# Second layer by pairs of feature chunks, and the product with the last weight by Strassen's seven block products

## The chip, the core and the metric

The kernel runs on one core of one Trainium2 chip. The metric is the device time of one execution in microseconds; three runs of the kernel before gave 1046.52 to 1047.0, median 1046.98. The engines are named as the profile names them: PE is TensorE (matmuls; PEld its weight loads), DVE is VectorE, ACT is ScalarE, POOL is GpSimd, SP the queue that issues most DMAs.

## What is computed

A channel attention over 6016 tokens of 256 channels feeds two feed-forward layers:

```
x = v @ softmax(normalised kT q / tau)          # 6016 x 256
h = x @ w_in;  g = h * sigmoid(1.702 h);  x = g @ w_out          # first layer, d_ff 2048
gate = sigmoid(x @ w_gate);  val = x @ w_val                     # second layer, d_ff 1536
out = (gate * val) @ w_out2                                      # 6016 x 256
```

The change is in the last two lines.

## The kernel before

**Tiles.** Tokens lie along the free dimension, in 12 blocks of 512 (block 11 has 384). Every fp32 value that goes into a large product is split into two fp16 halves, high and low, and a product is three matmuls (high by high, high by low, low by high) summed in PSUM. The intermediate `x` of a block is split into `vo`; the weights of the gate and the value are in `s_t`, in 12 chunks of 128 features.

**A unit of the second layer.** `gv_unit(b, j)` works on block b and feature chunk j. Gate and value of the chunk are a 2x2 block product (rows: gate, value; columns: the two token halves of w = 256; contraction: the two halves of the 256 channels), and `seven` makes it with seven block products in Winograd's form, so 21 matmuls of w columns. Between them ACT copies partial sums out of PSUM (L1045: one copy into the other bank, two into SBUF, `u2` and `u4`) and DVE adds two of them to the value's bank (L1050). ACT makes the sigmoid (L1408), DVE multiplies (L1414), and the result is split in two fp16 halves, `gh` (L1421 on ACT or L1423 on DVE) and `gl` (L1426 on DVE). The two gate banks come in turns from four (`rot`), the value's from two (`acc` 2 and 3).

**The last weight.** `o_unit(b, j)` multiplies the chunk by its 128 rows of the last weight: two output halves of 128 channels by three matmuls of 512 columns (L1012 to L1014, the helper `prod3`), summed over the 12 chunks of the block in the banks `acc` 0 and 1. After the last chunk ACT copies both banks out with the scale (L1461) and SP stores them (L1466).

**The order.** Nothing runs in the order in which it is written. Each piece of work is given to `Plan.op` with estimated costs, the keys it reads and writes, and the engines that may run it; `Plan.run` then places everything by estimated time and emits it, so each engine's order is fixed when the program is built. A piece with a higher rank number yields to a lower one when both could start; `plan.delay` adds to that rank, and products with the last weight get `FILL2` = 60. In the plan POOL and DVE never run together, except with DVE work marked `lone` (those with an operand in PSUM). Rings (`gf`, `g`: three slots each) bound how far ahead an engine may run. Per block DVE and ACT also prepare `vo` of the next block (`y_ops`, `right_ops`: L310, L313, L359, L362, L365).

Of the kernel before, what the change touches and what calls it, by code (L numbers as in the profile page):

```python
# [166 lines left out]
def fused_kernel(ctx, tc, q, k, vt, tau, w_in, w_o1, w_g, w_v, w_o2, outt):  # L167
# [28 lines left out]
    HSHIFT = VSHIFT = 2.0**-19  # L196
# [1101 lines left out]
    for (b, f0), (nm, src) in zip(W_AT, (("o2", w_o2), ("g", w_g), ("v", w_v))):  # L1298
# [69 lines left out]
    def scales2(e):  # L1368
# [7 lines left out]
        nc.vector.tensor_scalar(ko, ko, w_p2["o2"], 1.0 / TOP / VSHIFT, op0=ALU.mult, op1=ALU.mult)  # L1376
# [4 lines left out]
    def gv_unit(b, j):  # L1381
# [23 lines left out]
        k_g = ring("g")

        def sig(e):
            nc.scalar.activation(  # L1408
                out=T[kf][:, :n].rearrange("p (x w) -> p x w", x=2), in_=pair_ap(kx, w), func=AF.Sigmoid, scale=T[sk]
            )  # L1410

        def mul(e):
            v = T[kf][:, NB : NB + n]
            nc.vector.scalar_tensor_tensor(  # L1414
                out=v, in0=v, scalar=VSHIFT, in1=T[kf][:, :n], op0=ALU.mult, op1=ALU.mult
            )

        def hi(e):
            T[name] = [g_p.tile([P, 2, NB], F16, tag=x, name=x + name)[:, 0, :] for x in ("gh", "gl")]
            if e == "act":  # L1420
# [113 lines left out]
```

## Time and profile before

| | us |
|---|---|
| median of three runs | 1046.98 |
| span of the profiled execution, first to last instruction | 1044.5 |
| busy in that span: PE / DVE / ACT / POOL | 1035.2 / 788.7 / 698.7 / 30.9 |
| first layer's last block ends, second layer's first begins | about 521 to 531 |
| one full block of the second layer | 43.06 |

The profiled execution's own device time is not listed; its span is 2.5 us below the median of the three runs, and this is taken as what lies around it. PE's busy time counts overlapping records, so it shows where PE is never empty, not its speed; that is read from starts of matmuls.

### The profile page before, as it was taken

To read this page: it belongs to the slowest core of one execution; us is meant where nothing else is said; L and a number is where in the kernel's file an instruction comes from. 1 tells how busy PE (TensorE), PEld (TensorE's weight loads), DVE (VectorE), ACT (ScalarE), POOL (GpSimd) and SP (SyncE) were. 2 spreads that over 40 slices of the span, in tenths; PEclk is the share of its full clock that TensorE was granted. 3 is DMA by queue.
4 is the path that set the end of the run, shared out by engine and by line. 5 is a ranking of instruction groups with operands and counts; after the bars stand their busy time and mean duration, and the time that the engine had idled before them with its cause. 6 is when DMAs were issued, how large, how long until landed. Compare 5 with 4: busy or idle time off the path is not lost.

```text
span 1044.5 us, 18259 instructions
## 1 busy us (share of the span) xinstructions
PE 1035.2 (99%) x7169; PEld 715.4 (68%) x7169; DVE 788.7 (76%) x1454; ACT 698.7 (67%) x1387; POOL 30.9 (3%) x39
## 2 busy tenths in 40 slices
PE   9999999999999999999999999999999999999998
PEld 7744456666666666666777777777777777777776
DVE  6999999999888766766686676766767767676665
ACT  6798368787876656655666666666666666666665
POOL 0120100100000000000000000000000000000000
PEclk9999999999999999999999999999999999999999
DMA  9920223300000000000000000000000000000000
GB/s 351 400 104 21 81 78 110 136 23 21 21 2 21 21 2 16 1 1 1 2 2 1 22 1 21 21 1 21 2 21 21 1 21 1 21 21 1 22 21 16
DMA packets 14517, 43.63 MB, mean 42 GB/s; under 512 B 1504, under 2 KB 2784, under 8 KB 12768
## 3 DMA queue, kind: packets, MB, share of 16 engines
q1 hardware_dynamic: 13856, 41.56, 11.0%
q8 instruction: 56, 0.92, 0.4%
q10 hardware_dynamic: 576, 0.92, 0.3%
q14 instruction: 29, 0.24, 0.1%
HBM read 36.31 MB, written 6.16 MB: 41 GB/s over the span
## 4 chain that ended last, share of the span: by engine, by line
PE 93%; DMA 2%; DVE 2%; issue 2%; ACT 1%; POOL 0%; SPq 0%; ACTq 0%; POOLq 0%
PE ps L1036 47%; PE ps L1014 15%; PE ps L1013 15%; PE ps L1012 15%; PE ps L947 1%; DMA tau<-in_tau 1%; DMA m_t<-in_q 1%; PE ps L749 0%; DMA m_t<-in_k 0%; POOL full_in L523 0%; DVE s_t L313 0%; DVE gl L313 0%; DVE full_in L513 0%; DVE big L628 0%; ACT gh L310 0%
## 5 line engine op out<-in xcount | busy, mean ns | idle before, releaser
L1036 PE MATMUL ps<-vo,s_t 128*128 128x256 f16 (+1 forms) x3024 | 370.9, 270 | 0.6 <-ACT m_t L1045 0.6
L1036 PEld LDWEIGHTS <-s_t 128*128 128x128 f16 x3024 | 292.8, 98 | 91.2 <-issue 1.2
L1050 DVE TENSOR_TENSOR gf<-ps,m_t 128x256 f32<-128x256 f32 (+1 forms) x448 | 185.2, 415 | 140.7 <-PE ps L1036 102.9
L1045 ACT COPY m_t<-ps 128x256 f32<-128x256 f32 (+1 forms) x448 | 162.0, 363 | 98.5 <-PE ps L1036 97.1
L1036 PE MATMUL ps<-vo,m_t 128*128 128x256 f16 (+1 forms) x1680 | 217.8, 270 | 0.0
L1036 PEld LDWEIGHTS <-m_t 128*128 128x128 f16 x1680 | 162.6, 98 | 67.8 <-issue 1.0
L1408 ACT ACTIVATE gf<-ps,sgb 128x512 f32<-128x512 f32 (+1 forms) x144 | 97.6, 678 | 66.4 <-PE ps L1036 66.4
L1426 DVE TENSOR_TENSOR gl<-gf,gh 128x512 f16<-128x512 f32 (+1 forms) x144 | 97.9, 680 | 46.1 <-ACT gh L1421 43.5
L1013 PE MATMUL ps<-gl,wo 128*128 128x512 f16 (+1 forms) x348 | 130.2, 374 | 0.0
L1014 PE MATMUL ps<-gh,wo 128*128 128x512 f16 (+1 forms) x348 | 130.2, 374 | 0.0
L1012 PE MATMUL ps<-gh,wo 128*128 128x512 f16 (+1 forms) x348 | 130.2, 374 | 0.0
L1421 ACT CAST gh<-gf 128x512 f16<-128x512 f32 (+1 forms) x132 | 80.4, 609 | 71.7 <-PE ps L1014 71.5
L313 DVE SCALAR_TENSOR_TENSOR gl<-gf,sgi,gh 128x1024 f16<-128x1024 f32 (+1 forms) x87 | 109.0, 1254 | 4.4 <-ACT gh L310 3.8
L1414 DVE SCALAR_TENSOR_TENSOR gf<-gf 128x512 f32<-128x512 f32 (+1 forms) x144 | 98.0, 680 | 13.9 <-ACT gf L1408 0.6
L1013 PE MATMUL ps<-gl,wo_h 128*128 128x512 f16 (+1 forms) x288 | 107.9, 375 | 0.0
L1014 PE MATMUL ps<-gh,wo_l 128*128 128x512 f16 (+1 forms) x288 | 107.9, 375 | 0.0
L1012 PE MATMUL ps<-gh,wo_h 128*128 128x512 f16 (+1 forms) x288 | 107.9, 375 | 0.0
L1045 ACT COPY ps<-ps 128x256 f32<-128x256 f32 (+1 forms) x224 | 82.0, 367 | 16.5 <-PE ps L1036 15.2
L1014 PEld LDWEIGHTS <-wo 128*128 128x128 f16 x384 | 37.6, 98 | 43.6
L1203 DVE TENSOR_SCALAR gh<-gf,sgi 128x1024 f16<-128x1024 f32 (+1 forms) x62 | 45.7, 737 | 27.2 <-PE ps L1014 25.0
L1180 ACT ACTIVATE gf<-gf,sgs 128x512 f32<-128x512 f32 (+1 forms) x80 | 56.0, 708 | 11.5 <-DVE gf L1050 10.6
L1180 ACT ACTIVATE gf<-ps,sgs 128x512 f32<-128x512 f32 (+1 forms) x80 | 53.7, 672 | 9.3 <-PE ps L1036 8.9
(219 smaller groups left out, 982.9 us busy)
## 6 DMA issues: line engine op xcount, KB each, us to landing
v_raw<-in_vt SPq DMA_DIRECT2D x11, 512.0 KB, 5.2
out_t<-ob SPq DMA_DIRECT2D x22, 256.0 KB, 2.0
m_t<-in_k SPq DMA_DIRECT2D x9, 512.0 KB, 6.6
m_t<-in_q SPq DMA_DIRECT2D x9, 512.0 KB, 7.5
s_t<-in_w_o SPq DMA_DIRECT2D x3, 1024.0 KB, 4.9
s_t<-in_w_g SPq DMA_DIRECT2D x3, 1024.0 KB, 5.0
s_t<-in_w_v SPq DMA_DIRECT2D x3, 1024.0 KB, 4.8
big<-in_w_in SPq DMA_DIRECT2D x2, 1024.0 KB, 9.5
```

Source lines behind the costliest of these rows:

```text
L313: nc.vector.scalar_tensor_tensor(out=lo, in0=x, scalar=s, in1=h, op0=ALU.mult, op1=ALU.subtract)
L1012: nc.tensor.matmul(ps[:, :n], w_h, x_h, start=first, stop=False)
L1013: nc.tensor.matmul(ps[:, :n], w_h, x_l, start=False, stop=False)
L1014: nc.tensor.matmul(ps[:, :n], w_l, x_h, start=False, stop=last)
L1036: nc.tensor.matmul(dst, l, r, start=start and y == 0, stop=y == 2, skip_group_check=True)
L1045: op(lambda e: nc.scalar.copy(out=dst, in_=bank(key)[:, :w]), ("act", 0.1 + w / 1150), r=[key], w=[wk], after=after)
L1050: nc.vector.tensor_add(val(half), bank(kw)[:, :w], other)
L1180: nc.scalar.activation(out=dst, in_=pair_ap(kx, w) if x == 0 else dst, func=AF.Gelu_apprx_sigmoid, scale=T[sk][0])
L1408: nc.scalar.activation(out=T[kf][:, :n].rearrange("p (x w) -> p x w", x=2), in_=pair_ap(kx, w), func=AF.Sigmoid, scale=T[sk])
L1414: nc.vector.scalar_tensor_tensor(out=v, in0=v, scalar=VSHIFT, in1=T[kf][:, :n], op0=ALU.mult, op1=ALU.mult)
L1421: nc.scalar.copy(out=T[name][0][:, :n], in_=T[kf][:, NB : NB + n])
L1426: nc.vector.tensor_sub(T[name][1][:, :n], T[kf][:, NB : NB + n], T[name][0][:, :n])
```

## The change

`gv_pair(b, p)` takes two feature chunks (2p, 2p + 1) at once: each of the seven products is made for both chunks into the two halves of one PSUM bank (6 matmuls of 256 columns in a row), and each copy, add and sigmoid works on 512 columns, the product with the gate on 1024. One bank serves all first partial sums (`A_BANK`), one the values (`V_BANK`), and two take turns (`K_BANK`); `acc` 0 to 3 are all left to the last product.

In blocks 1 to 10, `o_pair(b, p)` treats the pair's product with the last weight as a 2x2 block product as well (rows: the two output halves; columns: the two token halves; contraction: the two chunks) and makes it with seven products of 256 columns, summed over the six pairs of a block in seven half banks. For that the pair's result is needed in seven forms: three quarters as they are (`pl`, split by L1548 on ACT and L1551 on DVE) and four sums (`t13`, `t2`, `t4`, `ts` in the trace; L1563, L1566, L1569), split again (L1586, L1589). The four sums of the weight are made once, during block 0 (`o2_sums`). At the end of a block ACT copies the seven sums out (L1687) and seven adds (`comb`, L1695) make the output. Blocks 0 and 11 (`PLAIN2`) keep the product of before, by pairs. `t2`, `t4` and `comb` may run on POOL.

```
-    def gv_unit(b, j):
+    def gv_pair(b, p):
...
+        t = wturn["n"] = 1 - wturn["n"]
+        ka, kx, kw = A_BANK, K_BANK[t], V_BANK
...
+                for f in range(2):
+                    j = 2 * p + f
+                    dst = bank(key)[:, f * w : (f + 1) * w]
+                    lh, ll = [late_pools()["S"][:, j * P // NB, y, a, j * P % NB : j * P % NB + P] for y in range(2)]
+                    for y, (l, r) in enumerate(((lh, rh), (lh, rl), (ll, rh))):
+                        nc.tensor.matmul(dst, l, r, start=start and f == 0 and y == 0, stop=y == 2, skip_group_check=True)
...
+        product(0, 0, ka, True)
+        copy(bank(kx)[:, : 2 * w], ka, kx)
+        product(1, 2, ka, False)
+        product(3, 5, kx, False)
+        copy(u2, kx, ku2)
+        product(4, 4, kw, True)
+        sig(1, ka)
+        product(6, 3, kx, False)
+        copy(u4, kx, ku4)
+        add(0, u4, ku4)
+        product(5, 1, kx, False)
+        product(2, 6, kw, False)
+        add(1, u2, ku2)
+        sig(0, kx)
...
+        op(hi_p, ("act", 0.12 + 0.69 * f), r=rg, w=[kp], after=late_after)
+        op(t13, either(2), r=rg, w=[kt])
+        op(t2, either(1), r=rg + [kt], w=[("t2", name)])
+        op(t4, either(1), r=rg + [kt, ("t2", name)], w=[("t4", name)])
+        op(lo_p, ("dve", 0.12 + 0.81 * f), r=rg + [kp], w=[("plo", name)])
...
+        op(hi_t, ("act", 0.12 + 0.9 * f), r=rt, w=[kg])
+        op(lo_t, ("dve", 0.12 + 1.08 * f), r=rt + [kg], w=[("glo", name)])
...
-    def o_unit(b, j):
+    def o_pair(b, p):
...
+            for x, (a, r, start) in enumerate(((0, 0, True), (1, 2, False), (3, 5, True), (6, 3, False),
+                                               (4, 4, True), (2, 6, False), (5, 1, True))):
+                product(a, r, x, start)
...
+        for k in (0, 3, 1, 2):
+            evac(k)
+        comb(M2, M1, M2)
+        comb(M6, M1, M6)
+        comb(M5, M6, M5)
+        comb(M6, M6, M7)
+        comb(M7, M5, M7)
+        comb(M4, M4, M6)
+        comb(M3, M3, M5)
...
-        for j in range(NF2):
-            gv_unit(b, j)
-            queue2.append((b, j))
+        for p in range(NP2):
+            gv_pair(b, p)
+            queue2.append((b, p))
...
-            elif len(queue2) > 1:
-                o_unit(*queue2.pop(0))
+            elif len(queue2) > LAG2:
+                o_pair(*queue2.pop(0))
...
+            if b == 0 and p >= NP2 - 3:
+                o2_sums(p - NP2 + 3, y_last)
```

Up to the first product of the second layer the order of every engine is the same as before.

DVE, kernel before, around the start of block 4 of the second layer (names carry block, chunk and a buffer number; `tt` and `vo` are `y_ops`):

```order
1008 L1414 SCALAR_TENSOR_TENSOR gf_4_0_7252<-gf_4_0_7252 128x512 [waits DVE_49]
1009 L1426 TENSOR_TENSOR gl_3_11_7286<-gf_3_11_7202,gh_3_11_7285 128x512 [waits Activation_49]
1010 L1050 TENSOR_TENSOR gf_4_1_7303<-ps,m_t 128x256 [waits DVE_49]
1011 L362 TENSOR_TENSOR tt<-big,tt 128x256
1012 L365 TENSOR_TENSOR tt<-big,tt 128x256 [waits DVE_49]
1013 L1050 TENSOR_TENSOR gf_4_1_7303<-ps,m_t 128x256 [waits PE_49]
1014 L1414 SCALAR_TENSOR_TENSOR gf_4_1_7303<-gf_4_1_7303 128x512 [waits DVE_49,Activation_49]
```

The same engine with the change, around the start of block 5 (names carry block and pair):

```order
1033 L1524 SCALAR_TENSOR_TENSOR gf_5_0_7774<-gf_5_0_7774,m_t 128x1024 [waits DVE_49]
1034 L314 SCALAR_TENSOR_TENSOR vo<-big,s_y_203,vo 128x768
1035 L1589 TENSOR_TENSOR gl_4_5_7836<-ts_4_5_7796,gh_4_5_7835 128x1024 [waits Activation_49]
1036 L1563 TENSOR_TENSOR ts_5_0_7870<-gf_5_0_7774 128x512 [waits DVE_49]
1037 L1493 TENSOR_TENSOR gf_5_1_7879<-ps,m_t 128x2x256 [waits Activation_49]
1038 L1551 TENSOR_TENSOR m_t<-gf_5_0_7774,m_t 128x768 [waits Activation_49]
1039 L1569 TENSOR_TENSOR ts_5_0_7870<-gf_5_0_7774,ts_5_0_7870 128x256 [waits Pool_49]
1040 L1493 TENSOR_TENSOR gf_5_1_7879<-ps,m_t 128x2x256 [waits PE_49]
1041 L366 TENSOR_TENSOR tt<-big,tt 128x256
1042 L1524 SCALAR_TENSOR_TENSOR gf_5_1_7879<-gf_5_1_7879,m_t 128x1024 [waits DVE_49,Activation_49]
1043 L1589 TENSOR_TENSOR gl_5_0_7906<-ts_5_0_7870,gh_5_0_7905 128x1024 [waits Activation_49]
```

A pair now takes, beside two adds and one multiplication, the sums `ts` and two splits; here `t2` of pair (5,0) went to POOL, and DVE's `t4` (row 1039) waits for it.

PE with the change, where the first products of pair (5,0) with the last weight stand (`s_t` rows are gate and value products, `m_t` and `gh`/`gl` rows products with the last weight):

```order
10217 L1472 MATMUL ps<-vo,s_t 128x256
10220 L1640 LDWEIGHTS wo_h
10221 L1640 MATMUL ps<-m_t,wo_h 128x256
10222 L1640 LDWEIGHTS wo_h
10223 L1640 MATMUL ps<-m_t,wo_h 128x256
10226 L1640 LDWEIGHTS wo_87
10227 L1640 MATMUL ps<-gh_5_0_7905,wo_87 128x256
10229 L1640 MATMUL ps<-gl_5_0_7906,wo_87 128x256
```

Counting L1472 rows, 42 to a pair, 198 of block 5 stand ahead of row 10227: four pairs and five products of the fifth. The first products from `gl` of pair (5,0) so come 3.7 pairs after that pair's own gate and value products.

POOL with the change, between two blocks (before, POOL had only one cross-partition maximum, L277, left to do in block 0):

```order
63 L1695 TENSOR_TENSOR m_t<-m_t 128x256 [waits DMAHW2_49]
64 L1695 TENSOR_TENSOR m_t<-m_t 128x256 [waits Activation_49]
65 L1569 TENSOR_TENSOR ts_3_3_7100<-gf_3_3_7015,ts_3_3_7100 128x256 [waits DVE_49]
66 L1569 TENSOR_TENSOR ts_3_5_7305<-gf_3_5_7202,ts_3_5_7305 128x256 [waits DVE_49,Activation_49]
67 L1569 TENSOR_TENSOR ts_4_0_7375<-gf_4_0_7299,ts_4_0_7375 128x256 [waits DVE_49,Activation_49]
68 L1566 TENSOR_TENSOR ts_4_1_7440<-gf_4_1_7351,ts_4_1_7440 128x256 [waits DVE_49,Activation_49]
```

All 70 `comb` adds and 37 of the 120 `t2` and `t4` are on POOL.

## Rows read from the trace of the kernel before

**Rows 1.** The page's chain of work that ended last, by engine.

```profile
PE 93%; DMA 2%; DVE 2%; issue 2%; ACT 1%; POOL 0%; SPq 0%; ACTq 0%; POOLq 0%
```

**Rows 2.** What PE waited for, 530 to 1030 us: in total, times, longest.

```profile
PE ps L1036 <- ACT m_t L1045: 0.6, 1, 0.6
```

**Rows 3.** The chain that ended last: start, length, once per block of the second layer.

```profile
595.81 3.61 PE ps L1036 x33
638.87 3.61 PE ps L1036 x33
```

**Rows 4.** Timeline of PE: start, us, what; two stretches without waits.

```profile
552.60 3.77 PE L1036 MATMUL ps<-vo,s_t 128*128 128x256 f16 x33
556.20 0.38 PE L1012 MATMUL ps<-gh,wo_h 128*128 128x512 f16 x1
...
703.52 0.38 PE L1012 MATMUL ps<-gh,wo_h 128*128 128x512 f16 x1
...
704.60 0.38 PE L1014 MATMUL ps<-gh,wo_l 128*128 128x512 f16 x1
```

**Rows 5.** Busy us by stretch: PE, PEld, DVE, ACT, POOL (instructions), clock, DMA.

```profile
160.00:280.00 120.00, 120.00 (x812) 79.14 (x810) 112.32 (x205) 96.38 (x178) 5.17 (x8) 1.00 0.17 56
360.00:480.00 120.00, 120.00 (x813) 79.25 (x811) 83.11 (x155) 72.69 (x142) 4.49 (x7) 1.00 0.02 4
595.80:638.90 43.10, 43.10 (x327) 31.73 (x325) 30.10 (x57) 28.23 (x63) 0.00 (x0) 1.00 0.04 13
```

**Rows 6.** Groups by shape: busy us, mean ns, then idle before.

```profile
L1050 DVE TENSOR_TENSOR gf<-ps,m_t 128x256 f32<-128x256 f32 x408 | 171.0, 421 | 129.1 <-PE ps L1036 97.0 <-ACT m_t L1045 24.6
L1008 DVE TENSOR_TENSOR m_t<-ms,m_t 128x1024 f16<-128x1024 f32 x4 | 4.9, 1216 | 0.0
L359 DVE TENSOR_TENSOR tt<-big 128x512 f32<-128x512 f32 x7 | 4.8, 682 | 0.0
L362 DVE TENSOR_TENSOR tt<-big,tt 128x256 f32<-128x256 f32 x7 | 2.9, 415 | 0.0
L313 DVE SCALAR_TENSOR_TENSOR vo<-big,s_y,vo 128x768 f16<-128x768 f32 x7 | 7.1, 1016 | 0.1
L1408 ACT ACTIVATE gf<-ps,sgb 128x512 f32<-128x512 f32 x132 | 90.6, 686 | 62.2 <-PE ps L1036 62.1
L1007 ACT CAST m_t<-ms 128x1024 f16<-128x1024 f32 x4 | 4.1, 1037 | 9.4 <-DVE ms L988 9.3
```

**Rows 7.** Timeline: two DVE instructions in a row, then a hand-over from PE to ACT to PE.

```profile
704.81 0.49 PE L1036 MATMUL ps<-vo,s_t 128*128 128x256 f16 x3
...
705.22 0.68 DVE L1426 TENSOR_TENSOR gl<-gf,gh 128x512 f16<-128x512 f32 x1
...
705.34 0.37 ACT L1045 COPY m_t<-ps 128x256 f32<-128x256 f32 x1 [0.36 <-PE ps L1036]
...
705.79 1.15 PE L1036 MATMUL ps<-vo,s_t 128*128 128x256 f16 x9
705.83 0.68 DVE L1414 SCALAR_TENSOR_TENSOR gf<-gf 128x512 f32<-128x512 f32 x1
```

**Rows 8.** Timeline near the start: two POOL multiplications, each with DVE's work beside it.

```profile
29.72 2.78 POOL L523 TENSOR_TENSOR full_in<-full_in,big 128x1024 f32<-128x1024 f32 x1 [17.12 <-DVE full_in L513]
...
29.55 3.50 DVE L729 TENSOR_TENSOR kacc<-kacc,sq 128x512 f32<-128x512 f32 x2
...
61.98 2.40 POOL L523 TENSOR_TENSOR full_in<-full_in,raw_in 128x1024 f32<-128x1024 f32 x1 [1.54 <-ACT m_t L310]
...
61.94 4.17 DVE L313 SCALAR_TENSOR_TENSOR m_t<-ps,rss,m_t 128x512 f16<-128x512 f32 x6
```

**Rows 9.** Timeline at the first layer's end, and at the program's end.

```profile
528.28 1.28 ACT L1408 ACT_TABLE_LOAD   x1
...
1038.00 0.33 PE L1012 MATMUL ps<-gh,wo_h 128*128 128x384 f16 x1
...
1040.11 0.33 PE L1013 MATMUL ps<-gl,wo_h 128*128 128x384 f16 x1
```

More of the change, by code (lines that the diff above doesn't have):

```diff
@@ L1357, in fused_kernel @@
             m_sums(SUMS_AT.index(step), [step_op[step]])
+        if b == NBLK - 1:
+            m_users += range(began, len(plan.ops))
         queue.append(step)
@@ L1405, in gv_unit @@
[L1405 to L1409, printed above, removed]
-            )
[L1412 to L1420, printed above, removed]
-                nc.scalar.copy(out=T[name][0][:, :n], in_=T[kf][:, NB : NB + n])
-            else:
-                nc.vector.tensor_copy(T[name][0][:, :n], T[kf][:, NB : NB + n])
@@ new lines, in copy, with quarters, pairs, add @@
+        def copy(dst, key, wk):
+            op(lambda e: nc.scalar.copy(out=dst, in_=bank(key)[:, : 2 * w]), ("act", 0.12 + 2 * w / 1180), r=[key], w=[wk],
+               after=late_after if wk[0] != "rot" else ())
+        def quarters(a, half):
+            return a[:, : 4 * w].rearrange("p (f x w) -> p f x w", f=2, x=2)[:, :, half, :]
+        def pairs(a):
+            return a[:, : 2 * w].rearrange("p (f w) -> p f w", f=2)
+        def add(half, other, ko):
+            def fn(e):
+                if half == 0:
+                    T[kf] = t_p.tile([P, 2 * NB], F32, tag="gf", name="gf" + name)
+                nc.vector.tensor_add(quarters(T[kf], half), pairs(bank(kw)), pairs(other))
+            op(fn, ("dve", 0.12 + 2 * w / 960), r=[kw, ko] + ([] if half == 0 else [kf]),
+               w=[kf] if half == 0 else [("val2", kf)], lone=True)
@@ new lines, in sig, with fn @@
+        def sig(half, key):
+            def fn(e):
+                nc.scalar.activation(out=quarters(sig_t[ks[1] % 2], half), in_=pairs(bank(key)), func=AF.Sigmoid, scale=T[sk])
+            op(fn, ("act", 0.16 + 2 * w / 1180), r=[key, sk] + ([ks] if half == 0 else []), w=[ks] if half == 1 else [("sig2", ks)],
+               after=late_after)
+        u2, u4 = u2_t[:, t, 0, : 2 * w], u2_t[:, t, 1, : 2 * w]
+        product(0, 0, ka, True)
+        copy(bank(kx)[:, : 2 * w], ka, kx)
+        product(1, 2, ka, False)
@@ new lines, in gv_pair, with hi_t @@
+        op(hi_p, ("act", 0.12 + 0.69 * f), r=rg, w=[kp], after=late_after)
[3 more added lines that the diff above has]
+        op(lo_p, ("dve", 0.12 + 0.81 * f), r=rg + [kp], w=[("plo", name)])
+        kg = ring("g")
+        def hi_t(e):
+            T[name] = [g_p.tile([P, 2, NB], F16, tag=x, name=x + name).rearrange("p f n -> p (f n)") for x in ("gh", "gl")]
+            nc.scalar.copy(out=T[name][0][:, : 4 * w], in_=T[kt][:, : 4 * w])
@@ L1480, in fused_kernel @@
             if queue:
-                y_unit(*queue.pop(0))
-                if not queue:
-                    y_max(NBLK - 1)
-                    y_scale(NBLK - 1)
-            elif len(queue2) > 1:
-                o_unit(*queue2.pop(0))
-            if j == 3 and b + 1 < NBLK:
+                began = len(plan.ops)
+                while queue:
+                    y_unit(*queue.pop(0))
+                y_last = list(range(began, len(plan.ops)))
+                y_max(NBLK - 1)
+                y_scale(NBLK - 1)
+            elif len(queue2) > LAG2:
+                o_pair(*queue2.pop(0))
```

225 lines of the change are left out of this document (185 added, 40 removed).

## Prediction

> **What bounds the kernel now.** I read the chain that ended last first: PE holds 93% of it and no other engine has more than 2% [rows 1]; the granted clock is 1.00, the 2.4 GHz level, in every stretch that I read [rows 5]. Next the waits of PE in the second layer: one, of 0.6 us, in 500 us [rows 2]. So PE is full there, and what counts is how fast its matmuls follow each other, not its busy time. The chain passes the same place once per block, 638.87 - 595.81 = 43.06 us apart [rows 3]. Where nothing waits, 33 matmuls of 256 columns start in 556.20 - 552.60 = 3.60 us, 109.1 ns each, and five of 512 columns in 704.60 - 703.52 = 1.08 us, 216 ns each [rows 4]. A block has 12 x 21 = 252 of the first and 12 x 6 = 72 of the second: 27.5 + 15.5 = 43.0 us. The block is its matmuls and nothing else. In the same block DVE is busy 30.10 of 43.10 us and ACT 28.23, POOL not at all [rows 5]: some 30% of room on either, and this is what the change spends.
>
> **PE: what is removed.** Per pair, 42 gate and value matmuls of 256 columns stay as they are, only in runs of six. Twelve matmuls of 512 columns with the last weight (12 x 0.2155 = 2.59 us, by what the period leaves for them) become 21 of 256 columns (21 x 0.1091 = 2.29 us). The new block has 6 x 63 = 378 matmuls of 256 columns, 378 x 0.1091 = 41.24 us, against 43.06: 1.82 us less. Ten blocks (1 to 10) do it: **-18.2 us**. Blocks 0 and 11 keep their matmuls: 0. More than this cannot come out, because the first layer's order is unchanged and PE has no idle time to give back but the 0.6 us of [rows 2].
>
> **ACT: what is added.** Per pair: three PSUM copies and two sigmoids of 512 (0.686 each, the price of the sigmoid), one split of 768 (no row; between the 0.686 of 512 and the 1.037 of 1024, taken as 0.85) and one of 1024 (1.037) [rows 6]: 5.3 us. Six pairs give 31.9; four copies at the block's end (three of 512 and one of 256, by the same prices at most 2.7) and the two splits for the next block (0.85 + 1.04 = 1.9) make 36.5 us, 89% of 41.24. Taken as hidden, since the stretch 160 to 280 us had ACT at 96.38 of 120 and PE lost nothing (below). Cost 0.
>
> **DVE: what is added.** Per pair: two adds of 512 from PSUM (0.42 for 256 in [rows 6]; 512 taken like the SBUF one, 0.68), the multiplication of 1024 (1.216), `t13` of 512 (0.682), `t2` and `t4` of 256 (0.415 each), `lo` of 768 (between 0.682 and 1.216; 0.95) and `lo` of 1024 (1.216): 6.25 us, 37.5 for six pairs. The preparation of the next block adds 0.682 + 2 x 0.415 + 1.016 + 1.216 = 3.7 [rows 6]. The same prices for the block of before (24 x 0.415 + 24 x 0.68 + 3.7) give 30.0, and [rows 5] shows 30.10, so I trust them. From 41.2 I take what the order puts on POOL, 37 x 0.415 / 10 = 1.5: **39.7 us** of records per block. Records overlap by some 0.07 us when the next instruction does not wait (a 0.68 us one is followed after 0.61 [rows 7]); with about 50 instructions a block the true need lies between 36.2 and 39.7 us, 88 to 96% of 41.24.
>
> Can PE stay full beside a DVE that busy? The trace has that case. From 160 to 280 us DVE is busy 112.32 of 120 us (94%) and PE starts 812 matmuls; from 360 to 480 us DVE is at 83.11 (69%) and PE starts 813 [rows 5]. The mix is the first layer's in both. So a static order of this planner held PE full at 94%, and I take DVE's added work as hidden.
>
> **POOL beside DVE.** This the trace of before does not show in the second layer. Each block gets 7 adds and 3.7 `t2` or `t4` of 256 elements. The nearest row is a POOL multiplication of 1024, 2.78 us, and it ran beside two DVE adds whose records took 3.50 us together [rows 8], where two such take 2 x 0.682 = 1.36: DVE stood still for some 2.1 us, nearly POOL's whole work. A second one, 2.40 us, ran beside six DVE splits that read PSUM, and these kept their pace, 4.17 / 6 = 0.70 us each for 512 elements. So DVE work with an operand in PSUM is not held up. A quarter of 2.78 us is 0.70 for 256 elements; with a fixed part it is more, and 0.75 is my estimate, bounded by 0.52 (a quarter of the 2.1) and 2.78 (no gain from fewer elements). 10.7 x 0.75 = 8.0 us of POOL per block. DVE is delayed by nothing, if all of it falls on DVE's PSUM adds (12 x 0.68 = 8.2 us a block) or its idle time, and by 8.0 us if none does. By this, DVE needs 38 + 0 to 8 = 38 to 46 us, with PE at 41.24. The planner kept the two engines apart in its order, so that DVE's instructions stand where it expected POOL to be done; I take a collision cost that reaches PE of 0.25 us per block, **+2.5 us**, and keep 0 and 46 - 41.2 = 4.8 us per block as the ends.
>
> The Trainium skill, "SBUF — State Buffer", section "Who interferes with whom", says that a VectorE instruction with two SBUF inputs contends with a GpSimd instruction that reads SBUF, and that one with at most one SBUF input does not. The 3.50 us agree with the first half and the 4.17 us with the second. By that rule alone every sum, split and multiplication of the new block can be held up and only the adds cannot, so the end with 8.0 us is the one to fear: 1077, worked out with the rivals.
>
> **Banks.** One bank now carries all first partial sums and one all values. The value's circle for a pair is product, add, product, add, 4 x 0.67 = 2.7 us, with four hand-overs. PE's three matmuls from 704.81 end at 705.30, ACT starts its copy at 705.34, ends at 705.71, and PE starts again at 705.79 [rows 7], so a hand-over is below 0.1 us where the receiver is free: 3.1 us of the 6.87 us that a pair takes. The circle decides only when DVE answers on average 0.9 us late. Taken as 0.
>
> **The slack of the last product.** Between a pair's last gate product and its products with the last weight lie add, multiplication, `t13`, `t2`, `t4`, `hi` and `lo`: 0.68 + 1.22 + 0.68 + 0.42 + 0.42 + 1.04 + 1.22 = 5.7 us, 6.4 with seven hand-overs. In the order they stand 3.7 pairs later for pair (5,0), 25 us. So PE has ready work in hand, and a late `lo` does not stop it; a late add does.
>
> **The start.** The last four feature chunks of the first layer now lie between products of the second in longer runs, and the load of the sigmoid's table (1.28 us on ACT [rows 9]) has copies for PE queued behind it; of it 0.6 us reached PE before. I add **+1 us** (0 to 3). The weight's sums in block 0 are 3 x (1.216 + 4 x 0.415 + 1.216) = 12.3 us on DVE, in a block whose own work is 6 x 3.8 + 3.7 = 26.5 of 43: hidden; without that room it would be at most 12.3.
>
> **The end.** Block 11's last product is as before, and 57 of its matmuls (13 of 384 columns in 1040.11 - 1038.00 = 2.11 us [rows 9], 0.162 each, 9.2 us) stand behind the last gate product, which needs add, multiplication and split, about 4 us. Cost 0. Stores go in four pieces of 128x256 per block, on a queue with little to do: 0.
>
> **The sum.** 1044.5 - 18.2 + 2.5 + 1 = 1029.8 us of span; with the 2.5 us by which the median of the runs lies above the span, **1032.3 us**.
>
> **Rivals.** *POOL and DVE collide for about half of POOL's work* (4 us): DVE needs 38 + 4 = 42 us a block, with the odd wait on top 42.3; the ten blocks give 10 x 0.76 = 7.6 back, and with +1 the time is 1040.4. For it: 8 us of POOL in a block with 3 us of spare DVE time. Against: the plan's own separation.
>
> *DVE becomes the bound and the kernel is slower.* Place: every block from 1 to 10, where the adds that free the value's bank queue behind held-up splits. It decides when more than 43.06 - 38 = 5.1 of POOL's 8 us hold DVE up, about two thirds. At three quarters it is 44 us a block, +9.4, and 1057; with all of it 46 us, 1077. For it: in [rows 8] nearly all of POOL's time was lost to DVE. Against: 8.2 us of adds from PSUM in a block that could lie beside POOL.
>
> *Single banks.* The Trainium skill, "Perfetto Trace Analysis", section "Matmuls", asks that independent groups rotate through different PSUM banks. As a mechanism of this kernel: if each of the 66 pairs of blocks 0 to 10 loses 0.3 us until the previous pair's second add has emptied the value's bank, 20 us go, and the time is 1052; at 0.1 us, 1039. Against it stand the 3.7 us of slack in the circle.
>
> **How the numbers follow.** Forecast (PE bound, 1028.8 to 1036): 0.58. Half collided (1036 to 1045): 0.20. DVE bound (1046 to 1077): 0.16. Banks (1036 to 1055): 0.06. The range 1028.5 to 1045 holds the first two and half of the last, 0.81. About 0.2%, 2.1 us, is what a measurement of this kernel can tell from no change. Faster: 0.58 + 0.20 + 0.02 = 0.80. Slower: 0.13 of the third case and 0.02 of the last, 0.15; the same: 0.05.
>
> **What would show it.** In the changed profile: blocks 41.3 to 41.6 us apart in PE's order, 378 matmuls of 256 columns in each; PE's waits below 0.5 us a block; DVE at 88 to 96% of a block, ACT at 84 to 89%, POOL at about 8 us. DVE records of `lo` or `ts` much longer than 1.22 and 0.42 us beside a POOL add would show the collision; waits of PE on DVE's L1493 that add up to over 1.8 us a block would make the prediction wrong. Waits at the first layer's end of more than 3 us would show the start mis-sized.

## The result and the profile after

The changed kernel takes 1027.76 us (median of four runs, 1027.24 to 1029.05); before took 1046.99 beside it. The ratio is 0.9819, with a 95% interval of 0.9807 to 0.9831, a gain of 19.2 us. The profiled execution took 1027.24 us, with a span of 1025.2 us. The forecast was 1032.3; the time lies 0.7 us below the lower end of its range. Most kernels here have single executions with a mean granted clock of 0.998 instead of 1.00 that take some 2 us longer (1029.05 against 1027.24 to 1028.10 here), so up to 2 us of a difference between two medians of four can be that.

The page of the changed kernel: busy time by engine, then the chain that ended last by engine (as [rows 1]), then the groups of the second layer's work. L1472 are the gate's and value's products, L1640 the seven block products of the last weight, L1493 DVE's two adds that read PSUM, L1480 ACT's copies out of PSUM, L1500 its sigmoids, L1695 the combinations.

```profile
PE 1016.8 (99%) x7709; PEld 767.9 (75%) x7709; DVE 875.7 (85%) x1377; ACT 736.6 (72%) x1193; POOL 122.2 (12%) x145
...
PE 91%; DVE 3%; DMA 2%; issue 2%; ACT 1%; POOL 0%; SPq 0%; ACTq 0%; POOLq 0%
...
L1472 PE MATMUL ps<-vo,s_t 128*128 128x256 f16 (+1 forms) x3024 | 362.0, 270 | 0.2 <-ACT m_t L1500 0.2
L1493 DVE TENSOR_TENSOR gf<-ps,m_t 128x512 f32<-128x512 f32 (+1 forms) x144 | 97.3, 676 | 37.2 <-PE ps L1472 31.8
L1480 ACT COPY m_t<-ps 128x512 f32<-128x512 f32 (+1 forms) x144 | 83.0, 576 | 38.7 <-PE ps L1472 34.7
L1695 POOL TENSOR_TENSOR m_t<-m_t 128x256 f32<-128x256 f32 x70 | 65.5, 949 | 67.3 <-ACT m_t L1687 65.1
```

What PE waited for in the second layer (in total, times, longest), as [rows 2], and the busy time of PE, PEld, DVE, ACT and POOL, as [rows 5]: the whole second layer, then two stretches inside it.

```profile
PE ps L1472 <- ACT m_t L1500: 0.2, 1, 0.2
...
521.68:1021.63 499.95, 499.70 (x4505) 436.37 (x4502) 444.34 (x607) 373.99 (x568) 92.03 (x107) 1.00 0.04 13
...
650.00:814.00 164.00, 164.00 (x1505) 147.00 (x1503) 150.19 (x204) 127.00 (x192) 36.39 (x42) 1.00 0.04 14
814.00:980.00 166.00, 165.99 (x1523) 148.66 (x1522) 151.28 (x203) 127.48 (x193) 35.95 (x41) 1.00 0.04 14
```

The second layer of before, from its first gate product to its last product:

```profile
521.53:1040.60 519.07, 518.44 (x3965) 383.55 (x3962) 357.63 (x684) 336.46 (x762) 0.64 (x1) 1.00 0.03 12
```

So the second layer went from 519.07 to 499.95 us, 19.1 less, and what lies around it from 525.4 to 525.2. The view of waits has PE waiting for 0.2 us in it. In the eight blocks of the two stretches DVE is busy 301.47 of 330 us (91%), ACT 254.49 (77%) and POOL 72.34, or 9.0 us in a block of 41.3.

The feared collision is there. The timeline of POOL, then that of DVE, at the end of a block:

```profile
922.71 3.94 POOL L1695 TENSOR_TENSOR m_t<-m_t 128x256 f32<-128x256 f32 x3
...
921.97 1.75 DVE L314 SCALAR_TENSOR_TENSOR vo<-tt,s_y,vo 128x1024 f16<-128x1024 f32 x1
923.64 1.75 DVE L1589 TENSOR_TENSOR gl<-ts,gh 128x1024 f16<-128x1024 f32 x1
925.30 0.68 DVE L1493 TENSOR_TENSOR gf<-ps,m_t 128x512 f32<-128x512 f32 x1
```

And a place without one:

```profile
934.11 0.73 POOL L1566 TENSOR_TENSOR ts<-gf,ts 128x256 f32<-128x256 f32 x1 [6.78 <-ACT m_t L1500]
...
933.88 0.68 DVE L1493 TENSOR_TENSOR gf<-ps,m_t 128x512 f32<-128x512 f32 x1
```

A POOL add of 256 elements takes 0.73 us beside a DVE add that reads PSUM, and neither is stretched. Of the three in the 3.94 us above, the first two lie beside DVE's work in SBUF and take 1.59 us each, the third lies beside L1493 and takes 0.72; `lo` (L1589) takes 1.75 instead of 1.22: 0.53 more. That is about the lower of the two bounds that the prediction set for one such add (0.52, a quarter of the 2.1 of [rows 8]). PE loses next to nothing by it. Why not is what the experiments are about.

### The profile page after: what moved, and what is told of

The parts are those of the page before. It is cut to its first block, busy times and chain, and to the rows that moved or that the text cites. A ratio compares the mean times of both kernels' runs of the same rounds, so it can differ in the third digit from the quotient of the medians.

```text
span 1025.2 us, 18922 instructions
## 1 busy us (share of the span) xinstructions
PE 1016.8 (99%) x7709; PEld 767.9 (75%) x7709; DVE 875.7 (85%) x1377; ACT 736.6 (72%) x1193; POOL 122.2 (12%) x145
## 4 chain that ended last, share of the span: by engine, by line
PE 91%; DVE 3%; DMA 2%; issue 2%; ACT 1%; POOL 0%; SPq 0%; ACTq 0%; POOLq 0%
PE ps L1472 31%; PE ps L1037 17%; PE ps L1640 13%; PE ps L1015 10%; PE ps L1014 10%; PE ps L1013 10%; PE ps L948 1%; DMA tau<-in_tau 1%; DVE gl L314 1%; DMA m_t<-in_q 1%; DMA m_t<-in_k 1%; DVE vo L314 0%; POOL full_in L524 0%; DVE gf L1051 0%; DVE s_t L314 0%
## 5 line engine op out<-in xcount | busy, mean ns | idle before, releaser
L1472 PE MATMUL ps<-vo,s_t 128*128 128x256 f16 (+1 forms) x3024 | 362.0, 270 | 0.2 <-ACT m_t L1500 0.2
L1472 PEld LDWEIGHTS <-s_t 128*128 128x128 f16 x3024 | 292.6, 98 | 38.2 <-issue 0.6
L1493 DVE TENSOR_TENSOR gf<-ps,m_t 128x512 f32<-128x512 f32 (+1 forms) x144 | 97.3, 676 | 37.2 <-PE ps L1472 31.8
L1500 ACT ACTIVATE m_t<-ps,sgb 128x512 f32<-128x512 f32 (+1 forms) x144 | 97.5, 680 | 41.4 <-PE ps L1472 40.5
L314 DVE SCALAR_TENSOR_TENSOR gl<-gf,sgi,gh 128x1024 f16<-128x1024 f32 (+1 forms) x87 | 109.1, 1255 | 4.2 <-ACT gh L311 3.6
L1046 ACT COPY m_t<-ps 128x256 f32<-128x256 f32 (+1 forms) x160 | 57.5, 364 | 74.4 <-PE ps L1037 73.2
L1480 ACT COPY m_t<-ps 128x512 f32<-128x512 f32 (+1 forms) x144 | 83.0, 576 | 38.7 <-PE ps L1472 34.7
L1051 DVE TENSOR_TENSOR gf<-ps,m_t 128x256 f32<-128x256 f32 (+1 forms) x160 | 65.3, 414 | 42.6 <-ACT m_t L1046 25.6
L1524 DVE SCALAR_TENSOR_TENSOR gf<-gf,m_t 128x1024 f32<-128x1024 f32 (+1 forms) x72 | 88.2, 1229 | 1.9
L1589 DVE TENSOR_TENSOR gl<-ts,gh 128x1024 f16<-128x1024 f32 x60 | 74.4, 1241 | 3.4 <-ACT gh L1586 3.3
L1640 PEld LDWEIGHTS <-wo 128*128 128x128 f16 x720 | 70.3, 98 | 8.0
L1640 PE MATMUL ps<-gh,wo 128*128 128x256 f16 x360 | 76.1, 273 | 0.0
L1695 POOL TENSOR_TENSOR m_t<-m_t 128x256 f32<-128x256 f32 x70 | 65.5, 949 | 67.3 <-ACT m_t L1687 65.1
L1015 PEld LDWEIGHTS <-wo 128*128 128x128 f16 x384 | 37.6, 98 | 43.6
L1586 ACT CAST gh<-ts 128x1024 f16<-128x1024 f32 x60 | 62.7, 1046 | 6.1 <-DVE ts L1569 3.6
```

The costliest lines, as they stand in the source:

```text
L314: nc.vector.scalar_tensor_tensor(out=lo, in0=x, scalar=s, in1=h, op0=ALU.mult, op1=ALU.subtract)
L1015: nc.tensor.matmul(ps[:, :n], w_l, x_h, start=False, stop=last)
L1472: nc.tensor.matmul(dst, l, r, start=start and f == 0 and y == 0, stop=y == 2, skip_group_check=True)
L1480: op(lambda e: nc.scalar.copy(out=dst, in_=bank(key)[:, : 2 * w]), ("act", 0.12 + 2 * w / 1180), r=[key], w=[wk], after=late_after if wk[0 ...
L1493: nc.vector.tensor_add(quarters(T[kf], half), pairs(bank(kw)), pairs(other))
L1500: nc.scalar.activation(out=quarters(sig_t[ks[1] % 2], half), in_=pairs(bank(key)), func=AF.Sigmoid, scale=T[sk])
```

## The experiments

Theory A: PE is the bound throughout, and what the change adds to DVE, ACT and POOL is hidden, collisions included. Against it stand a gain that comes from elsewhere (the pairs and their full banks), collisions that do reach PE, and a DVE that is the bound itself.

**pairs_only.** What the pairs do without Strassen's products.

```diff
-T_BY, T_PEN, E_BY, E_PEN, LAG2, PLAIN2 = ("dve", "pool"), 0.0, ("dve", "pool"), -1.0, 2, (0, 11)
+T_BY, T_PEN, E_BY, E_PEN, LAG2, PLAIN2 = ("dve", "pool"), 0.0, ("dve", "pool"), -1.0, 2, tuple(range(12))
```

> The changed kernel with all 12 token blocks on the plain products (PLAIN2 = all blocks): pairs of features on full banks stay, Strassen's products do not run (the weight sums of block 0 are still formed). Theory A (TensorE is the bound throughout; the columns of the products with the last weight are what the change saves, and the pairs take away only the short stalls of the last block, 0.7 us, and 0.4 us at the layer's start): 1045.5 to 1046.3 us, blocks 43.0 to 43.1 us apart. Rival B (the pairs themselves give a share of the gain of 19 us, through fuller banks): below 1042. Rival C (the start costs 1 us, as the prediction's sum had it): 1048.

1045.25 us, ratio 0.9985 (0.9976 to 0.9993) to before: 1.8 us less, 0.25 us more than A's expectation allowed; nearly all of the gain is the products'. The second layer of this kernel:

```profile
522.69:1040.28 517.59, 517.35 (x3965) 383.56 (x3962) 322.21 (x403) 325.47 (x488) 0.35 (x1) 1.00 0.03 12
```

It is 519.07 - 517.59 = 1.5 us shorter than in before, and Strassen's products take away another 517.59 - 499.95 = 17.6 us, 1.76 in each of ten blocks. Where half of the 1.5 us was, the timeline of PE shows in block 11, first before, then the changed kernel: twelve products of 192 columns.

```profile
1026.68 1.24 PE L1036 MATMUL ps<-vo,s_t 128*128 128x192 f16 x12
```

```profile
1010.24 1.15 PE L1472 MATMUL ps<-vo,s_t 128*128 128x192 f16 x12
```

PE lost 0.09 us inside such a run and waited for nothing that the view of waits names: it leaves short waits out. All that PE loses can be read from the starts of its products. A stop is the time by which the step from one product to the next is longer than in an unbroken run (0.109 us for 256 columns, 0.0825 for 192, 0.162 for 384, 0.216 for 512). In the second layer the stops add up to 1.89 us in before, 0.41 in pairs_only and 0.63 in the changed kernel. So they are the whole 1.5 us: the one at the layer's start (the wait of 0.6 us of [rows 2]) went from 0.79 to 0.40, nine in block 11 with 0.77 together are gone, and so are two at 667 and 789 us with 0.28 together.

**no_pool and all_pool.** Everything that may go to either engine on DVE alone, then on POOL alone (the first and the second new line); the planner makes a new order for each.

```diff
-T_BY, T_PEN, E_BY, E_PEN, LAG2, PLAIN2 = ("dve", "pool"), 0.0, ("dve", "pool"), -1.0, 2, (0, 11)
+T_BY, T_PEN, E_BY, E_PEN, LAG2, PLAIN2 = ("dve",), 0.0, ("dve",), -1.0, 2, (0, 11)
+T_BY, T_PEN, E_BY, E_PEN, LAG2, PLAIN2 = ("pool",), 0.0, ("pool",), -1.0, 2, (0, 11)
```

> The changed kernel with every addition of the second layer on VectorE (no GpSimd). VectorE is busy 37.6 us of 41.1 in a block of the changed kernel; some 3.4 two-input additions of 0.42 us and 7 of 0.42 us per block come to it, and about 1 us of lengthened instructions goes, so about 41 us of 41.3. Theory A (collisions with GpSimd are hidden, VectorE's remaining slack is what is spent): 1028 to 1034 us, with TensorE waits for VectorE's parts in some blocks. Rival D (collisions of GpSimd with VectorE do reach TensorE in the changed kernel): faster than the changed kernel by 1 to 2.5 us, 1025 to 1027.

> The changed kernel with all four differences of a pair and all seven combinations on GpSimd (120 + 60 + 70 additions instead of 34 + 70): GpSimd some 24 us of a block instead of 9, VectorE about 30 us of its own work. Theory A (a GpSimd addition beside VectorE's two-input work stretches both, but both lie in slack): 1027 to 1029.5 us. Rival D (collisions reach TensorE as the prediction's sum had it, 2.5 us per 8 us of GpSimd a block): +7 us, about 1035; as its rival had it, 1045 and more. A second way to lose under A: the chain of a pair becomes longer than the slack of the last product, which shows as TensorE waits on line 1640 for VectorE or ScalarE.

no_pool took 1033.78 us, 6.0 more than the changed kernel, inside A's expectation: without POOL there is no collision, and it is slower all the same. PE's waits there are not for DVE's parts, as expected, but for ACT's copies (2.4 of 2.8 us listed from block 1 on). all_pool took 1047.50, 19.7 more, which A did not expect. What PE waited for in all_pool, from block 1 on, and POOL's groups between 650 and 980 us:

```profile
PE ps L1472 <- ACT ps L1480: 7.0, 4, 1.8
PE ps L1472 <- DVE gf L1493: 3.1, 8, 0.7
PE ps L1640 <- DVE gl L1589: 2.1, 4, 0.5
...
L1563 POOL TENSOR_TENSOR ts<-gf 128x512 f32<-128x512 f32 x46 | 78.4, 1705 | 73.8 <-DVE gf L1524 35.6 <-ACT m_t L1480 17.6 <-ACT m_t L1500 11.1
L1566 POOL TENSOR_TENSOR ts<-gf,ts 128x256 f32<-128x256 f32 x45 | 53.7, 1193 | 3.1
```

So POOL's work does reach PE when there is more of it. Load, collisions and order change together here; the next runs take them apart.

**dve_more1, load_only, plan_only.** A quarter of a pair's last split is made twice. dve_more1 has both edits below; load_only has the first alone, so that the planner doesn't know and every engine keeps the changed kernel's order; plan_only has the second alone.

```diff
         def lo_t(e):
             nc.vector.tensor_sub(T[name][1][:, : 4 * w], T[kt][:, : 4 * w], T[name][0][:, : 4 * w])
+            nc.vector.tensor_sub(T[name][1][:, : 1 * w], T[kt][:, : 1 * w], T[name][0][:, : 1 * w])
...
-        op(lo_t, ("dve", 0.12 + 1.08 * f), r=rt + [kg], w=[("glo", name)])
+        op(lo_t, ("dve", 0.12 + 1.08 * f + 0.12 + 1 * 0.27 * f), r=rt + [kg], w=[("glo", name)])
```

> The changed kernel with a quarter of the low part of a pair's differences formed twice on VectorE (one more 128x256 subtraction, 0.42 us, in each of 60 pairs; the result is unchanged): VectorE 37.6 + 2.5 = 40.1 us of a block of 41.3. Theory A (what is not TensorE's work is hidden up to a full engine): no change, 1027.5 to 1028.7 us. Rival E (VectorE's slack is already used up where it matters, in the last steps of a pair): +0.42 us for each pair, about 1053, or a good part of it, above 1033.

> dve_more1's extra subtraction (0.42 us on VectorE in each of 60 pairs), but with the planner told the old duration, so that the order of all instructions on all engines is the changed kernel's. It tells the load of dve_more1 (1051.8 us, +24 on the changed kernel) from the other order that the planner made of it. Theory F (the slack of VectorE is smaller than the 0.42 us per pair, since it stands still for TensorE's banks within the pair: VectorE and TensorE hand work to each other in turn): 1045 to 1053 us, nearly +0.42 us per pair. Theory G (the order of dve_more1 cost the time; VectorE's 3.5 idle us a block take 2.5 more): 1028 to 1032 us.

> The counterpart: the planner is told 0.42 us more for that subtraction, as in dve_more1, but the subtraction is not doubled; the order moves, the work is the changed kernel's. Theory F (load): 1027 to 1031 us. Theory G (order): 1045 us or more.

dve_more1 took 1051.82 us (+24.1), load_only 1040.13 (+12.4), plan_only 1042.46 (+14.7). A failed here, in the form in which DVE's idle time is its room: 0.42 us a pair is 2.5 of the 3.6 us in which DVE stands idle in a block, and in load_only half of it reached PE. Neither F nor G held either: the load alone and the order alone each cost some 13 us. PE's waits from block 1 on, in load_only, then in plan_only:

```profile
PE ps L1472 <- DVE gf L1493: 6.3, 12, 1.4
PE ps L1472 <- ACT m_t L1500: 0.5, 1, 0.5
```

```profile
PE ps L1472 <- ACT m_t L1500: 6.1, 8, 1.0
PE ps L1640 <- DVE m_t L1551: 1.6, 7, 0.2
```

In load_only PE waits for the adds that free the value's bank, the wait that the prediction named as the one to look for. The view lists half of it: by the starts of its products PE stops for 12.8 us in all, 10.2 of them until such an add has ended. In plan_only, with the changed kernel's work (only three `t2` went from POOL to DVE), a sigmoid and the splits come too late. It happens at one place in each of seven blocks and costs some 2 us each time, here at 770 us (DVE, ACT, PE):

```profile
767.04 1.28 DVE L314 SCALAR_TENSOR_TENSOR vo<-tt,s_y,vo 128x1024 f16<-128x1024 f32 x1
...
769.48 0.83 ACT L1548 CAST m_t<-gf 128x768 f16<-128x768 f32 x1 [1.49 <-DVE gf L1524]
770.22 0.68 ACT L1500 ACTIVATE m_t<-ps,sgb 128x512 f32<-128x512 f32 x1
...
770.96 0.82 PE L1472 MATMUL ps<-vo,s_t 128*128 128x256 f16 x6 [0.96 <-ACT m_t L1500]
```

The multiplication L1524 stands behind DVE's L314, which prepares the next block; the split L1548 waits for it, and the sigmoid that PE needs stands behind that split on ACT. The order of the changed kernel is therefore part of its time: another one, made by the same planner from one duration that was 0.39 us longer, loses 14.7 us.

**load_half and load_double.** The dose at the changed kernel's order: 128 elements (the first line) and 512 (the second) in place of load_only's 256.

```diff
+            nc.vector.tensor_sub(T[name][1][:, : w // 2], T[kt][:, : w // 2], T[name][0][:, : w // 2])
...
+            nc.vector.tensor_sub(T[name][1][:, : 2 * w], T[kt][:, : 2 * w], T[name][0][:, : 2 * w])
```

> As load_only (the changed kernel's order on every engine), with an extra VectorE subtraction of 128x128 instead of 128x256 in each of 60 pairs: by the step from 256 to 512 elements (0.42 to 0.68 us) about 0.28 us. Theory H (VectorE has a slack of fixed size in each pair and beyond it every nanosecond counts; load_only's +12.4 us for 60 x 0.42 us makes it 0.21 us a pair): +4 us, about 1032. Rival I (no slack: a share of about half of any load on VectorE reaches TensorE): +8 us, about 1036.

> As load_only, with an extra subtraction of 128x512 (0.68 us) in each of 60 pairs. Theory H (a slack of 0.21 us a pair): 60 x 0.47 = +28 us, about 1056. Rival I (half of the load): +20 us, about 1048.

1032.86 and 1055.14 us, near H's 1032 and 1056. The records of the extra instruction are 0.292, 0.425 and 0.692 us long, and the next DVE instruction starts 0.209, 0.343 and 0.610 us after it (medians). The three kernels are 5.1, 12.4 and 27.4 us over the changed kernel, which is 0.085, 0.206 and 0.456 us for each of 60 pairs. The difference is 0.124, 0.137 and 0.154 us. The second layers alone, which the medians hold beside everything else, in the same order:

```profile
523.77:1027.69 503.92, 501.57 (x4505) 436.28 (x4502) 462.36 (x667) 374.08 (x568) 96.74 (x107) 1.00 0.04 13
...
522.74:1034.84 512.10, 504.53 (x4505) 436.08 (x4502) 472.57 (x667) 374.89 (x568) 97.38 (x107) 1.00 0.04 13
...
523.79:1051.70 527.91, 507.71 (x4505) 435.99 (x4502) 489.50 (x667) 375.20 (x568) 98.92 (x107) 1.00 0.04 12
```

They are 3.97, 12.15 and 27.96 us longer than the changed kernel's 499.95, which is 0.066, 0.203 and 0.466 us a pair, and the difference is 0.143, 0.140 and 0.144: the same for all three doses. So DVE has some **0.14 us of slack a pair** at this place and in this order, 0.8 us in a block, and beyond it every nanosecond counts. Its 3.6 idle us a block are not slack. More than half of them it waits for PE's products, 16.2 of 28.5 us from 650 to 980 us in the changed kernel:

```profile
DVE gf L1493 <- PE ps L1472: 16.2, 22, 1.6
```

**pe_less.** What the next saving on PE would bring; this kernel leaves out the low-weight term of three of the seven block products.

```diff
-                    for y, (l, r) in enumerate(((lh, rh), (lh, rl), (ll, rh))):
+                    terms = ((lh, rh), (lh, rl), (ll, rh))[: 2 if x in (0, 2, 4) else 3]
+                    for y, (l, r) in enumerate(terms):
...
```

> What the next saving of the same size on TensorE would bring: the third of the three 16-bit terms is left out of three of the seven block products (18 of 126 products with the last weight a block, so the output loses accuracy); the order of what is left is the changed kernel's. TensorE: 18 x 0.1093 = 1.97 us a block less, 19.7 us in ten blocks. Theory A alone (TensorE is the only bound): about 1008 us. Theory H (VectorE has 0.21 us of slack a pair, 1.3 us a block, and becomes the bound): about 1015 us. Rival I (VectorE and TensorE in turn, half reaches): about 1018 us.

1014.49 us: 13.3 of 19.7 us came out, near H's 1015. That is 1.3 us a block, where the doses leave 0.8, and what holds PE back then is not DVE alone:

```profile
650.00:814.00 164.00, 163.45 (x1489) 145.32 (x1488) 155.74 (x212) 132.05 (x200) 38.43 (x43) 1.00 0.04 14
```

DVE went from 150.19 to 155.74 of 164 us, 95%, and ACT from 127.00 to 132.05. By the starts of its products PE stops for 5.8 us behind the layer's start: 2.9 of them end with one of DVE's adds L1493, and 2.7 with a copy or a sigmoid of ACT, which mostly stand behind ACT's own splits. H's number came out, its bound only in half.

**pool_twice.** POOL's additions done twice (`t2` and the combinations are shown, `t4` is done likewise; `dump` is a scratch tile) at the unchanged order of the other engines.

```diff
+            if e == "pool":
+                nc.gpsimd.tensor_sub(s(2), q(2), s(0))
             eng(e).tensor_sub(s(2), q(2), s(0))
...
+                if eg == "pool":
+                    nc.gpsimd.tensor_add(dump[:, :w], e(a), e(c))
```

> Each of GpSimd's additions of the second layer done twice (34 of a pair's differences and 70 combinations; the second copy of a combination goes to a scratch tile), with the planner told nothing, so that the order on TensorE, VectorE and ScalarE is the changed kernel's: GpSimd some 18 us of a block instead of 9, twice the collisions with VectorE. Theory A (GpSimd's collisions with VectorE are hidden by slack): no more than +2 us, 1028 to 1030. The prediction's step (0.25 us per block for 8 us of GpSimd): +2.5 us, about 1030. Rival D (they reach TensorE once the slack is used): VectorE loses about as much as it lost already in the changed kernel, 0.8 us a block, against a slack of 1.3: still about 1028 to 1030 by H; with no slack, 1036 and more.

1077.25 us, 49.5 more than the changed kernel: every theory missed by far. The waits of PE, the longest one of ACT from block 1 on, and the timeline of POOL, then of DVE and ACT, at one place (line numbers are up to seven higher; L1473 are the gate's and value's products, L1481 the copies, L1574 is `t4`, L1591 the high part, L1494 the adds):

```profile
PE ps L1473 <- ACT m_t L1481: 18.9, 20, 4.1
PE ps L1473 <- DVE gf L1494: 13.5, 13, 2.4
...
ACT gh L1591 <- POOL ts L1574: 34.1, 20, 4.8
...
907.59 0.72 POOL L1573 TENSOR_TENSOR ts<-gf,ts 128x256 f32<-128x256 f32 x1 [4.29 <-DVE ts L1569]
908.39 1.59 POOL L1574 TENSOR_TENSOR ts<-gf,ts 128x256 f32<-128x256 f32 x1
...
908.15 1.25 DVE L1525 SCALAR_TENSOR_TENSOR gf<-gf,m_t 128x1024 f32<-128x1024 f32 x1
909.32 0.94 DVE L363 TENSOR_TENSOR tt<-big,tt 128x256 f32<-128x256 f32 x1
910.01 1.05 ACT L1591 CAST gh<-ts 128x1024 f16<-128x1024 f32 x1 [2.75 <-POOL ts L1574]
```

The first `t4` falls beside the PSUM add and takes 0.72 us. The second meets the multiplication L1525, takes 1.59, and the DVE instruction behind takes 0.94 in place of 0.42. But that is not what costs most: ACT waits 2.75 us for POOL with the high part, and its copies that free PE's banks stand behind it in its queue. DVE's low part waits for that high part in turn (19.0 us from 650 to 980 us), with adds behind it. (The granted clock was 0.99 and 0.98 in the two stretches of that time, worth at most some 5 of the 49.5 us.) So a late POOL add costs by what queues behind its reader; the changed kernel shows ACT waiting 2.5 us for `t4` in all. This run doesn't tell what a collision costs, and the next two were made for that.

**no_comb and no_comb_load.** The seven combinations of a block are cut to two of 256 columns, in the changed kernel and in load_only (most of the output's combination is left out).

```diff
-                (nc.gpsimd if eg == "pool" else nc.vector).tensor_add(e(out), e(a), e(c))
+                (nc.gpsimd if eg == "pool" else nc.vector).tensor_add(e(out)[:, :2], e(a)[:, :2], e(c)[:, :2])
```

> GpSimd's seven combinations of each of ten blocks are cut to two columns of 256 (most of the output's combinations are left out); the order on TensorE, VectorE and ScalarE is the changed kernel's. It takes away the collisions that stretched VectorE's instructions by some 9.5 us in ten blocks of the changed kernel. Theory H (TensorE is the bound there and the collisions lie in VectorE's slack): no change, 1027.3 to 1028.5 us. Rival D (collisions reach TensorE): 1018 to 1025 us.

> The same cut in load_only (0.42 us more on VectorE in each of 60 pairs, 1040.1 us). There the combinations stretched VectorE's instructions by 15.7 us in ten blocks. Theory H (beyond the slack every microsecond on VectorE counts, a stretched one too): most of load_only's 12.4 us comes back, 1028 to 1032 us. Rival J (the stretched instructions stand where VectorE would have waited for TensorE anyway, so a collision costs nothing even when VectorE is the bound): 1038 to 1040 us.

no_comb took 1027.37 us, its span is 1025.2 us as in the changed kernel. Its DVE:

```profile
650.00:814.00 164.00, 164.00 (x1505) 147.00 (x1503) 146.64 (x205) 126.94 (x192) 18.71 (x42) 1.00 0.04 14
814.00:980.00 166.00, 166.00 (x1525) 148.83 (x1523) 146.70 (x203) 127.50 (x193) 19.40 (x41) 1.00 0.04 14
```

DVE is busy 293.34 us with the same instructions that took 301.47: the combinations stretch them by 8.1 us in eight blocks, 1.0 a block, and PE hardly notices: its only stop that goes with them is one of 0.17 us, behind an L1493 at 963 us. The 36 `t2` and `t4` on POOL are still there; none of them takes longer than 0.735 us in the changed kernel. no_comb_load took 1031.74, 8.4 us less than load_only: where DVE has no slack left, the combinations cost 0.84 us a block, about half of the 15.7 us in ten blocks by which they stretch DVE's instructions there. So they have a price, and the changed kernel pays it out of slack. H holds, D and J don't.

**last_block and lag1.** A version that might have been faster (the first new line), and one with less slack (the second).

```diff
-T_BY, T_PEN, E_BY, E_PEN, LAG2, PLAIN2 = ("dve", "pool"), 0.0, ("dve", "pool"), -1.0, 2, (0, 11)
+T_BY, T_PEN, E_BY, E_PEN, LAG2, PLAIN2 = ("dve", "pool"), 0.0, ("dve", "pool"), -1.0, 2, (0,)
+T_BY, T_PEN, E_BY, E_PEN, LAG2, PLAIN2 = ("dve", "pool"), 0.0, ("dve", "pool"), -1.0, 1, (0, 11)
```

> The changed kernel with Strassen's products in the last block of 384 tokens too (PLAIN2 = block 0 alone). TensorE's columns: 72 products of 384 columns (0.1625 us) become 126 of 192 (0.0825 us), 11.7 - 10.4 = 1.3 us less. The end: the changed kernel has 3.6 us from the last product to the end of the span; with the combinations one ScalarE copy and up to three additions (0.33 us each at 192 columns) stand before the last store instead of the one copy, about +1 us. Theory A: 1026.5 to 1028.3 us, no change to a gain of 1 us. A rival (the combinations stand on the tail with all seven additions and the slow ones on GpSimd): 1029 to 1031 us.

> The changed kernel with the products of the last weight one pair behind the gate's products instead of two (LAG2 = 1). The prediction put the slack of these products at 3.7 pairs. If a slack of that size is there, 1027.5 to 1029 us. If the chain of a pair (sigmoid 0.68, product 1.23, differences 0.68 + 0.42 + 0.42, high part 1.05, low part 1.24, together 5.7 us of a pair's 6.9 without any queueing) uses it, TensorE waits on line 1640 in most pairs, 1 us or more each: above 1060 us.

last_block took 1036.83 us, 9.1 more. Its last block, PE's longest waits at the end of it, then its end in the chain that ended last:

```profile
980.62:1027.20 46.58, 42.42 (x452) 39.15 (x450) 39.48 (x60) 29.68 (x53) 9.95 (x13) 0.98 0.05 15
...
PE ps L1640 <- DVE gl L1589: 1.6, 2, 0.8
PE ps L1640 <- ACT gh L1586: 0.9, 2, 0.5
...
1026.29 0.59 ACT m_t L1687
...
1027.01 0.60 POOL m_t L1695
...
1029.59 1.09 POOL m_t L1695 x2
```

The block takes 46.6 us where the changed kernel takes 40.8 from its first gate product to the last product. Most of that is lost behind the last gate product, which ends at 1019 us: the products of the last pairs wait for their high and low parts, six stops with 4.6 us together, and no gate product is left to lie between. (In the last 3.2 us of the block the granted clock was 0.64, too.) Then five combinations on POOL stand one behind the other at the end: the span ends 6.2 us after the last product, not 3.6. My expectation had left the first out altogether, and the second was its rival. lag1 took 1030.13 us, 2.4 more. PE waits 0.2 us on L1640 in it, so the slack of the last product is there, as the prediction had it. The longer waits are for ACT's copies, 0.9 us, in an order that the planner made anew; how much of the 2.4 us is the order's is not shown.

## Why the prediction was right in direction and too high

| term of the sum | predicted, us | measured, us | from |
|---|---|---|---|
| span before | 1044.5 | 1044.5 | |
| products of ten blocks on PE | -18.2 | -17.6 | pairs_only to the changed kernel, second layer |
| pairs: start, block 11, elsewhere | +1, 0, 0 | -0.4, -0.8, -0.3 | before to pairs_only, stops of PE in the second layer |
| POOL beside DVE | +2.5 | 0 (at most 0.2, within the -17.6) | no_comb: same span |
| before and behind the second layer | 0 | -0.2 | spans less second layers |
| span after | 1029.8 | 1025.2 | |
| outside the span | 2.5 | 2.0 | the profiled execution; the median is 0.5 above it |

**The bound** was read rightly: PE is full in the second layer, before and after, and its matmuls' time is the gain. The products' -18.2 was 0.6 too much: 256-column products start 0.1093 us apart on average in the changed kernel's second layer (3988 pairs of starts), not 0.1091, which is 0.08 us in the 378 of a block; the 43.06 us that they were set against were measured.

**The step that failed in the sum is the term for POOL beside DVE**, +2.5. The collision happens, at 1.0 us of DVE a block and about the price of one add that the bound gave. What reached PE was 0.2 us at most in the whole layer. I compared DVE's need with PE's 41.24 us and then took a value between the ends that no row supported; no_comb and no_comb_load show the price and that slack covers it. The rival with half of POOL's work collided had the stretching four times too large (4 us a block) and falls; so does the slower one. The Trainium skill, "SBUF — State Buffer", section "Who interferes with whom", held in both halves: beside L1493, which reads one operand from PSUM, a POOL add kept its 0.73 us, and beside two-SBUF work both engines were held up.

**The second failed step** is "More than this cannot come out ... PE has no idle time to give back but the 0.6 us". The view of waits leaves short ones out; block 11 had stops of 0.09 us in PE's own row, which the pairs' order doesn't have, and outside the start they were 1.05 us in all. With it the start's +1 had the wrong sign: the stop there shrank from 0.79 to 0.40 us. This step and the collisions are 2.5 us each of the 4.6 by which the span was forecast too long; the products' 0.6 goes the other way.

**Banks**: the rival falls; PE waits 0.2 us in the whole layer. **DVE**: 88 to 96% predicted, 91% measured, and the reading behind it (hidden, because 94% was hidden at 160 to 280 us in [rows 5]) came out right by 0.14 us a pair, which was luck. It was not safe: load_only at 95 to 96% loses 12.4 us and plan_only loses 14.7 with the changed kernel's work. A busy share in another stage said nothing about where DVE's instructions stand in this one. The check of DVE's prices was in part chance as well: 30.0 is a sum of records, 30.10 is busy time, which counts overlaps once, and the records of that block add up to 31.3. **ACT**: 84 to 89% predicted, 77% measured. A PSUM copy of 512 takes 0.585 us and I had priced it like the sigmoid, 0.686, which is 1.9 of the 4.7 us a block; most of the rest is overlap, since the records add up to 34.4 us a block and the busy time is 31.8. **POOL**: 8.0 us a block predicted, 9.0 measured, the difference being its own stretching (36 `t2` and `t4` ran on it by the trace, not 37).

What stays open: why pe_less finds 1.3 us of slack a block where the doses find 0.8, and what lag1's 2.4 us are made of.

## What to carry to other kernels

Beside a full engine, the idle time of another is not its slack. Put a small extra instruction into the inner loop with the order held fixed, at two or three sizes: the part that costs nothing is the slack at that place, here 0.14 us of a pair's 0.6 idle. A collision or a late result is then priced by whether its engine is inside that slack, and by what queues behind the instruction that waits. Read what the full engine loses from the starts of its instructions: the view of waits showed about half of it in load_only. When one engine's saving has brought the others close to it, the next saving on the first brings only part of itself: 13.3 of 19.7 us here.

## What the runs showed of the hardware

A 128x256 POOL add that starts during a DVE instruction with both inputs in SBUF ends some 0.6 us after that instruction, and the next DVE instruction in SBUF is then late: 1.59 us in place of 0.73 on POOL, 0.94 in place of 0.42 on DVE. The loss of DVE per POOL add was up to some 0.53 us, and the same for a 1.22 us and a 0.42 us instruction. Beside a DVE add with one input in PSUM a POOL add kept its 0.73 us and the DVE add its 0.68.
